# Two more units of the fifth group as seven products, their weight sums earlier, and other PSUM banks for the last two spectral chunks

## The chip, the cores and the metric

The kernel runs on one core of a Trainium2 chip. The core has a matrix engine (TensorE, "PE" in the profile, its weight loads "PEld"), a vector engine (VectorE, "DVE"), a scalar engine (ScalarE, "ACT"), GpSimd ("POOL") and a DMA-issuing queue (SyncE, "SP"). Each engine works through its own instructions in the order in which they stand; engines wait for each other with semaphores. The metric is the device time of one execution in microseconds. The kernel before takes 408.13 us (median of three runs, 408.11 to 408.33).

## The reference

The input x has 2048 tokens of 448 numbers. After a layer norm, two branches are added to it.

```
x  = A_x
xn = _layernorm(x, axis=-1)
A  = irfft2(rfft2(xn) * (w_r + 1j * w_i))          # over tokens and channels
h  = _gelu(_layernorm(xn, axis=-1) @ w1)           # 448 -> 448
hs = concatenate(four quarters of h, shifted by +1, -1, +2, -2 tokens) @ w2
x1 = xn + hs
B  = x1 + _gelu(_layernorm(x1, axis=-1) @ w3) @ w4 # 448 -> 1792 -> 448
out = x + A + B
```

## The kernel before

**Tiles and stages.** Tokens lie in 16 blocks `b` of 128, in the tiles `xt0` to `xt7` (two blocks each), which also collect the result. Products are made in half precision with a high and a low half of each factor, so that each product is three passes (`PASS`): high by high, high by low of the second factor, low of the first factor by high. A first stage makes h and x1 (`w1_unit`, `w2_tile`, `ln2`). Then come the two long parts, which are interleaved: the channel MLP (`mlp`), and the spectral branch, in order `do_fold` and `step1` (transform over channels), 16 chunks of frequencies (`chunk_a`, `chunk_b`, `chunk_z`, `chunk_c`), and the inverse transform of 16 blocks (`gather_u`, `inv_a`, `inv_b`).

**The MLP.** It goes by groups G = 0 to 7 of 256 tokens and, in each, by seven units fp, each of which is 256 of the 1792 hidden columns. `front(G, fp)` makes the hidden values: 22 matmuls into one PSUM bank `pw3_Gfp` (L400, `pw` in the profile), then a gelu on ACT (L726) and the two halves `hf` on ACT and DVE (L728, L729). `back(G, fp)` multiplies by w4: 12 matmuls of 448 columns into the two banks `acc` of the group (L808). The banks of the fronts, tag "mm", are two. `mlp` issues fronts one or two units ahead of backs.

**Units as seven products.** For the units in the table `SEVEN` the back is a two-by-two block product with seven half-width products in place of eight (`seven`, L763): 7 x 3 = 21 matmuls of 224 columns (L778). Three of the seven go into `acc`, four into two further banks per group, `side` (tag "sp" in the fifth group). The front of such a unit is `sums` (L733): gelu into a tile `g` (L738), two DVE additions (L740, L741), and the two halves `hz` on ACT and DVE (L744, L745). The tile `g` has two buffers and `hz` has three; a buffer is written again only when every reader of its earlier content is done. The weights also need sums: `w4_sums(j)` (L749) loads w4's rows of unit pair j by a DMA, makes four DVE additions (L757) and splits the result into halves on ACT (L280) and DVE (L281) into `w4t[j]`. Its places: j = 1 overwrites hidden inputs that groups 0 and 1 read, j = 2 and 3 those that groups 2 and 3 read. When the units of the group are done, DVE adds `side` and `acc` to `xt` (L786, L815).

**The spectral chunks.** Chunk c: `pp` (L622) into a bank of tag "tr", halves `pf` (L629, L630); `px` (L639) into a bank of tag "sp", then `te` (ACT L644, DVE L645, L646), `z` on POOL (L648), halves `zb` (L655, L656), and `pu` (L667) into a bank of tag "sp", from which ACT and DVE write `y1` (L670, L671). Tags "sp" and "tr" have two banks each. The inverse gathers `U` from `y1` (L680), makes `pe` (L688) in "tr", a chain of DVE steps (L695 to L699) with halves `vh` (L701, L702), then `py` (L709) in "sp", and adds it to `xt` (L711).

**What sets the order.** The order on each engine is not written out: a scheduler takes the ready instruction of highest priority, by its own estimate of times. MLP fronts and backs run at the lowest priority (`FILL`), so that they fill PE while the spectral branch waits. `behind(...)` makes an instruction follow others. Once built, the order is fixed.

Of the kernel before, what the change touches and what calls it, by code (L numbers as in the profile page):

```python
# [12 lines left out]
F32 = mybir.dt.float32  # L13
# [25 lines left out]
AFTER = [[], [3], [4], [5], [6], [7], [], []]  # L39
EVAC, FILL = 0, 100000  # L40
DH = D // 2
SEVEN = {5: [0, 4, 5], 6: [0, 4, 5, 1, 2, 3], 7: [0, 1, 2, 4, 5]}
ORD = {G: list(range(7)) for G in range(5)} | {5: [1, 2, 3, 6, 0, 4, 5], 6: [0, 4, 5, 1, 2, 3, 6],
                                               7: [0, 1, 2, 4, 5, 3, 6]}

ME = [0, 224] + list(range(2, 224, 2))
# [79 lines left out]
def body(tc, nc, x, wf, w1, w2, w3, w4, c_g, c_n, c_small, out):  # L126
# [14 lines left out]
    def pool(name, bufs=1, side="left", space=None):  # L141
        kw = dict(name=name, bufs=bufs, reuse_waits="tile")
        if space is not None:
            kw["space"] = space
        else:
            kw["side"] = side
        cm = tc.tile_pool(**kw)
        opened[name] = cm
        return cm.__enter__()

    def close(name):
        opened.pop(name).__exit__(None, None, None)
# [3 lines left out]
    def bank(tag, name):  # L156
        return ps.tile([128, 512], F32, tag=tag, bufs=2, name=name)

    pc = pool("pc")
    px = pool("px")  # L160
# [213 lines left out]
    @contextlib.contextmanager  # L374
    def behind(*key):
        key = key if len(key) > 1 else key[0]
        with contextlib.ExitStack() as st:
            for i in after[key]:
                st.enter_context(tc.issue_after(i))
            yield  # L380
# [141 lines left out]
    def finish(b):  # L522
        t = xb(b)
        if b < 2:
            t = row()[:, :D]
            SY.dma_start(t, xv[:, at_token(b)])
            V.scalar_tensor_tensor(out=t, in0=xb(b), scalar=p12, in1=t, op0=ALU.mult, op1=ALU.add)
        SY.dma_start(ov[:, at_token(b)], t)
# [54 lines left out]
    def w_scale_end():  # L583
        t = pc.tile([128, 4], F32, name="wt")
        V.tensor_reduce(out=t[:, 0:1], in_=wm, axis=AX.X, op=ALU.max)
        pt = bank("sp", "wpt")
        T.transpose(pt[0:1, 0:128], t[:, 0:1], ident)
        V.tensor_reduce(out=t[0:1, 1:2], in_=pt[0:1, 0:128], axis=AX.X, op=ALU.max)
        V.tensor_scalar(out=t[0:1, 1:2], in0=t[0:1, 1:2], scalar1=2.0 ** -20, scalar2=None, op0=ALU.max)
        pb = bank("sp", "wpb")  # L590
        T.matmul(pb[:, 0:1], ones[0:1], t[0:1, 1:2], start=True, stop=True)
        e = pc.tile([128, 3], I32, name="we")
        V.tensor_copy(out=t[:, 2:3], in_=pb[:, 0:1])
        V.tensor_single_scalar(e[:, 0:1], t.bitcast(I32)[:, 2:3], 0x7F800000, op=ALU.bitwise_and)
        V.tensor_single_scalar(e[:, 1:2], e[:, 0:1], 0x7F800000, op=ALU.bitwise_xor)
        V.tensor_scalar(out=sc[:, 0:1], in0=e.bitcast(F32)[:, 1:2], scalar1=ZPRE, scalar2=None, op0=ALU.mult)
        for h in range(2):
            V.tensor_scalar(out=sc[64 * h:64 * h + 64, 2:3], in0=sc[64 * h:64 * h + 64, 0:1], scalar1=2.0 * h - 1.0,
                            scalar2=None, op0=ALU.mult)
        V.tensor_scalar(out=sc[:, 1:2], in0=e.bitcast(F32)[:, 0:1], scalar1=2.0 ** -21 / (ZPRE * UPRE * VPRE),  # L600
                        scalar2=s12[:, 0:1], op0=ALU.mult, op1=ALU.mult)
        V.tensor_scalar(out=sc[:, 3:4], in0=sc[:, 1:2], scalar1=p12, scalar2=None, op0=ALU.mult)
# [30 lines left out]
    def chunk_b(c):  # L633
        w, k, _ = stream[c]
        pf = pfs.pop(c)
        px_ = bank("sp", f"px{c}")
        for h in range(2):
            for n, (pi, gi) in enumerate(PASS):
                T.matmul(px_[:, DF * h:DF * h + DF], k[:, gi, h], pf[:, pi, h], start=n == 0, stop=n == 2)  # L639
        src = px_[:, :2 * DF]  # L640
        o = stage(f"te{c}", 6 * DF, c % 2)
        e, t = o[:, :2 * DF], o[:, 2 * DF:].rearrange("p (a n) -> p a n", a=2)
        for h in range(2):
            A.activation(out=e[64 * h:64 * h + 64], in_=px_[64 - 64 * h:128 - 64 * h, :2 * DF], func=AF.Copy)  # L644
        V.scalar_tensor_tensor(out=t[:, 0], in0=src, scalar=sc[:, 0:1], in1=w[:, 0], op0=ALU.mult, op1=ALU.mult)  # L645
        V.scalar_tensor_tensor(out=t[:, 1], in0=e, scalar=sc[:, 2:3], in1=w[:, 1], op0=ALU.mult, op1=ALU.mult)  # L646
        z = pst.tile([128, 2 * DF], F32, tag="z", bufs=2, name=f"z{c}")
        P.tensor_tensor(out=z, in0=t[:, 0], in1=t[:, 1], op=ALU.add)  # L648
        zs[c] = z
# [8 lines left out]
    def chunk_c(c):  # L658
        _, _, k = stream.pop(c)
        zh = zb[c % 2]  # L660
        pu = bank("sp", f"pu{c}")
        for par in range(2):
            for h in range(2):
                d = pu[:, 256 * par:256 * par + 256].rearrange("p (q k) -> p q k", k=8)[:, :, 4 * h:4 * h + 4]
                for n, (zi, ki) in enumerate(PASS):
                    o = (2 * zi + h) * DF + 113 * par
                    T.matmul(d, zh[:, o:o + 128], k[:, ki, h].rearrange("p (q k) -> p q k", k=4), start=n == 0, stop=n == 2)  # L667
        src = pu[:113].rearrange("p (q n) -> p q n", q=4)
        d = [Y1[:113, p, :, c].rearrange("p q b k -> p q (b k)") for p in range(2)]
        A.activation(out=d[0], in_=src, func=AF.Copy, scale=UPRE)  # L670
        V.scalar_tensor_tensor(out=d[1], in0=src, scalar=UPRE, in1=d[0], op0=ALU.mult, op1=ALU.subtract)  # L671
# [44 lines left out]
    def front(G, fp, tag):  # L716
# [5 lines left out]
        with prio(EVAC):  # L722
            if fp in SEVEN.get(G, ()):
                hs[G, fp] = sums(G, fp, pm)
# [24 lines left out]
    def w4_sums(j, part):  # L749

        t = part.rearrange("p (k n) -> p k n", n=DH)
        SY.dma_start(t.rearrange("p (f k) n -> p f (k n)", f=2), w4v[:, 2 * j:2 * j + 2])

        def go():
            for o, i, k, op in ((3, 3, 1, ALU.subtract), (1, 1, 0, ALU.subtract),
                                (0, 3, 0, ALU.add), (2, 2, 0, ALU.subtract)):
                V.tensor_tensor(out=t[:, o], in0=t[:, i], in1=t[:, k], op=op)  # L757
            split_w(w4t[j][:, 0], w4t[j][:, 1], t, s4)
        return go
# [3 lines left out]
    def seven(G, fp, end):  # L763
        h = hs.pop((G, fp))
        lead, last = fp == SEVEN[G][0], fp == SEVEN[G][-1]
        if lead:
# [5 lines left out]
        t2, t1, t4, t3 = ([w4t[fp][:, i, k] for i in range(2)] for k in range(4))  # L772
        begins = fp == ORD[G][0]
        for blk, to, b, new in ((2, m1, w(0, 0), lead), (4, a1[:, 0:DH], w(1, 0), begins), (1, a2[:, 0:DH], t4, begins),
# [13 lines left out]
    def back(G, fp):  # L788
        first, end = fp == ORD[G][0], fp == ORD[G][-1]
        if first:  # L790
# [3 lines left out]
        h = None  # L794
        if fp in SEVEN.get(G, ()):
            seven(G, fp, end)
        else:
            h = hs.pop((G, fp))
        for i in range(2):
# [3 lines left out]
            for r, to in parts if h is not None else ():  # L803
                with behind("m", G, fp) if G == 7 and end and ("m", G, fp) in after else contextlib.nullcontext():
                    for f in (2 * fp, 2 * fp + 1):
                        for n, (hi, wi) in enumerate(PASS):
                            o = 256 * (f % 2) + 128 * i
                            m = T.matmul(to, h[:, hi, o:o + 128], w4p[0][:, wi, f, r],  # L808
                                         start=first and f % 2 == 0 and n == 0, stop=end and f % 2 == 1 and n == 2,
                                         skip_group_check=G in SEVEN)  # L810
                after["m", G, fp] = (m.ins,)
# [8 lines left out]
    def mlp(Gs, hook=None, ahead=1, tags=("mm",)):  # L820
        with prio(FILL):
            todo = [(G, fp) for G in Gs for fp in ORD[G]]
            done = 0
            for n, (G, fp) in enumerate(todo):
                while done < min(n + 1 + (ahead if todo[n] != (7, 5) else 1), len(todo)):
                    front(*todo[done], tags[done % len(tags)])
                    if hook:
                        with prio(EVAC):
                            hook(*todo[done])
                    done += 1  # L830
                back(G, fp)
# [57 lines left out]
    n = 2  # L889
# [148 lines left out]
    close("pfd")  # L1038
    with behind("m", 2, 3):
        w_scale_end()  # L1040
    pst = pool("pst", side="right")
    zb = [pst.tile([128, 4 * DF + 16], F16, name=f"zb{i}") for i in range(2)]
    for i in range(2):
# [10 lines left out]
            chunk_c(i - 3)  # L1054
    close("pst")
    mlp(range(3, 5))
    pv = pool("pv", side="right")
    bs = [*range(8), *range(12, 16), *range(8, 12)]
    for n in range(17):
        if n in (0, 8):  # L1060
            gather_u(n)
        if n < 16:
            inv_a(bs[n])
        if n:
            b = bs[n - 1]
            inv_b(b)
            if b < 10:
                finish(b)
    close("pa2")
    pz = pool("pz")  # L1070
    LATE = [(1, 5, 0), (2, 5, 5), (3, 6, 4)]

    def w4_late(G, fp):
        for n, (j, *at) in enumerate(LATE):
# [33 lines left out]
```

## Time and profile before

| | |
|---|---|
| median of three runs | 408.13 us |
| the profiled execution, its own time | 408.05 us |
| span of its instructions | 406.3 us |
| PE busy | 399.9 us (98%) |
| DVE busy | 333.6 us (82%) |
| ACT busy | 255.1 us (63%) |

The span counts from the first to the last instruction; 1.75 us lie around it. Times in rows are from the span's start. A matmul's end is modelled, and the next one starts before it, so what a matmul costs PE is read from the distance of starts, not from its duration. "idle before" is time in which the engine did nothing before an instruction, with what ended it.

### The profile page before, as it was taken

What the parts mean: (1) busy time and instruction counts of PE and PEld (TensorE: products, weight loads), DVE (VectorE), ACT (ScalarE), POOL (GpSimd) and SP (SyncE); (2) the same over time, 40 slices, a digit from 0 to 9 for tenths busy, and PEclk for the clock granted to TensorE, in tenths of its full rate; (3) what the DMA queues carried; (4) which work ended last, traced back from release to release, by engine and by line L of the source; (5) the groups of instructions that cost most, each with busy time, mean ns of one, the idle gap of its engine ahead of it and who ended that gap; (6) DMA issues with size and microseconds to landing.
All of it is one profiled execution on the core that took longest, in us unless ns stands there. A gap on an engine that the chain in (4) does not pass through costs nothing.

```text
span 406.3 us, 8732 instructions
## 1 busy us (share of the span) xinstructions
PE 399.9 (98%) x3391; PEld 297.2 (73%) x3391; DVE 333.6 (82%) x702; ACT 255.1 (63%) x433; POOL 100.4 (25%) x158
## 2 busy tenths in 40 slices
PE   8999999999999999999999999999999999999996
PEld 3555555865667877777878878777677779998995
DVE  5898799898947887988698888965999999965645
ACT  4788889874568857655698878853354544353431
POOL 6859910111146946500021111110000000000000
PEclk9999999999999999999999999999999999999999
DMA  8978975567489661637256556510011023100101
GB/s 280 389 272 160 249 152 138 122 121 163 95 225 266 234 191 46 219 95 185 72 144 164 162 142 161 139 27 2 24 69 70 24 90 92 47 2 2 45 2 45
DMA packets 54596, 52.07 MB, mean 128 GB/s; under 512 B 35678, under 2 KB 48542, under 8 KB 54556
## 3 DMA queue, kind: packets, MB, share of 16 engines
q1 hardware_dynamic: 54556, 51.53, 46.0%
q8 instruction: 26, 0.43, 0.4%
q14 instruction: 14, 0.11, 0.1%
HBM read 38.28 MB, written 3.67 MB: 103 GB/s over the span
## 4 chain that ended last, share of the span: by engine, by line
PE 87%; POOL 5%; DMA 2%; DVE 2%; ACT 2%; issue 1%; SPq 0%; POOLq 0%; ACTq 0%
PE pw L400 33%; PE acc L808 23%; PE pw L478 6%; PE side L778 4%; PE acc L778 3%; PE pu L667 3%; PE ps L567 3%; PE pe L688 2%; PE pp L622 2%; PE px L639 2%; PE py L709 2%; PE pw L420 2%; DMA w1s<-w 1%; POOL xt L336 1%; DMA h<-x2mem 1%
## 5 line engine op out<-in xcount | busy, mean ns | idle before, releaser
L400 PE MATMUL pw<-x2mem,w3p 128*128 128x256 f16 x1232 | 151.3, 273 | 0.0
L400 PEld LDWEIGHTS <-w3p 128*128 128x128 f16 x1232 | 118.9, 98 | 19.3
L808 PE MATMUL acc<-w4p,hf 128*128 128x448 f16 (+1 forms) x516 | 104.4, 348 | 0.0
L808 PEld LDWEIGHTS <-hf 128*128 128x128 f16 x516 | 50.1, 98 | 37.6
L726 ACT ACTIVATE pw<-pw,pe 128x512 f32<-128x512 f32 x42 | 27.4, 654 | 26.8 <-PE pw L400 26.6
L729 DVE SCALAR_TENSOR_TENSOR hf<-pw,h,hf 128x512 f16<-128x512 f32 x42 | 31.3, 746 | 12.9 <-ACT hf L728 12.7
L478 PE MATMUL pw<-w2p,h 128*128 128x448 f16 x176 | 35.8, 353 | 0.9 <-DMA h<-x2mem 0.9
L420 PE MATMUL pw<-w1p,xT 128*128 128x448 f16 x176 | 34.9, 352 | 0.1
L648 POOL TENSOR_TENSOR z<-te 128x450 f32<-128x450 f32 x16 | 15.7, 983 | 70.8 <-DVE te L646 65.9
L728 ACT ACTIVATE hf<-pw,h 128x512 f16<-128x512 f32 x42 | 28.9, 687 | 5.0 <-PE acc L808 4.0
L478 PEld LDWEIGHTS <-h 128*128 128x128 f16 x176 | 17.0, 98 | 17.0 <-DMA h<-x2mem 2.0
L744 ACT ACTIVATE hz<-g,h 128x896 f16<-128x896 f32 x14 | 14.6, 1044 | 23.1 <-DVE g L741 23.1
L420 PEld LDWEIGHTS <-xT 128*128 128x128 f16 x176 | 17.1, 99 | 16.1 <-DVE xT L394 0.4
L778 PEld LDWEIGHTS <-hz 128*128 128x128 f16 x294 | 28.3, 98 | 0.6
L629 ACT ACTIVATE pf<-pp 64x450 f16<-64x450 f32 x32 | 17.4, 544 | 12.5 <-DVE pf L630 9.7
L630 DVE TENSOR_TENSOR pf<-pp,pf 64x450 f16<-64x450 f32 x32 | 19.9, 622 | 5.1 <-ACT pf L629 4.7
L745 DVE SCALAR_TENSOR_TENSOR hz<-g,h,hz 128x896 f16<-128x896 f32 x14 | 16.1, 1148 | 6.8 <-ACT hz L744 6.8
L550 POOL TENSOR_TENSOR f<-xr 128x452 f32<-128x452 f32 x16 | 19.7, 1251 | 0.6
L558 DVE TENSOR_TENSOR xh<-f,xh 128x452 f16<-128x452 f32 x16 | 14.3, 916 | 5.7 <-ACT xh L557 5.7
L644 ACT ACTIVATE te<-px 64x450 f32<-64x450 f32 x32 | 17.3, 541 | 1.2 <-PE px L639 0.6
L738 ACT ACTIVATE g<-pw,pe 128x512 f32<-128x512 f32 x14 | 9.6, 683 | 11.3 <-PE pw L400 11.3
L547 POOL TENSOR_TENSOR xr<-xf 128x452 f32<-128x452 f32 x8 | 9.2, 1156 | 22.3 <-issue 16.4
(188 smaller groups left out, 705.7 us busy)
## 6 DMA issues: line engine op xcount, KB each, us to landing
wc<-wf SPq DMA_DIRECT2D x32, 225.0 KB, 3.7
wl<-wf SPq DMA_DIRECT2D x8, 450.0 KB, 4.3
xt<-x SPq DMA_DIRECT2D x8, 448.0 KB, 7.1
xf<-x SPq DMA_DIRECT2D x8, 448.0 KB, 4.6
loads<-x SPq DMA_DIRECT2D x7, 448.0 KB, 4.0
out<-xt SPq DMA_DIRECT2D x13, 224.0 KB, 1.9
w3raw<-w SPq DMA_DIRECT2D x3, 896.0 KB, 10.8
gn<-c_g SPq DMA_DIRECT2D x16, 128.0 KB, 3.0
```

What stands on the lines that cost most here:

```text
L400: T.matmul(ps_out, wp[:, wi + t, cols], xT[:, xi + t, tok], start=t == 0 and wi + xi == 0, stop=t == 3 and wi == 4)
L420: m = T.matmul(pm[:, :D], xTs[g][:, xi + t, 128 * i:128 * i + 128], w1p[:, wi + t], start=t == 0 and p == 0, stop=t == 3 and p == 2)
L478: T.matmul(pm[:, :D], h[:, k], w2p[:, w], start=n == 0, stop=n == 10)
L550: P.tensor_tensor(out=f[:, :, k:k + 2].rearrange("p b s d -> p s b d"), in0=u[:, :, 0], in1=u[:, :, 1], op=op)
L629: A.activation(out=hi, in_=src, func=AF.Copy)
L630: V.tensor_tensor(out=lo, in0=src, in1=hi, op=ALU.subtract)
L644: A.activation(out=e[64 * h:64 * h + 64], in_=px_[64 - 64 * h:128 - 64 * h, :2 * DF], func=AF.Copy)
L726: A.activation(out=pm, in_=pm, func=AF.Gelu_apprx_tanh, scale=r3)
L728: i = A.activation(out=h[:, 0], in_=pm, func=AF.Copy, scale=h3)
L729: j = V.scalar_tensor_tensor(out=h[:, 1], in0=pm, scalar=h3, in1=h[:, 0], op0=ALU.mult, op1=ALU.subtract)
L778: m = T.matmul(to, h[:, hi, 128 * blk:128 * blk + 128], b[wi], start=new and n == 0, stop=n == 2 and (last if blk in (2, 5, 3, 0) else end ...
L808: m = T.matmul(to, h[:, hi, o:o + 128], w4p[0][:, wi, f, r], start=first and f % 2 == 0 and n == 0, stop=end and f % 2 == 1 and n == 2, sk ...
```

## The change

- `SEVEN[5]` gets the units 1 and 2: five units of the fifth group go as seven products. `ORD[5]` puts the two plain units first (3, 6), then 0, 4, 5, 1, 2.
- Half sums of w4 for j = 1 are made in the third group, behind its unit 1, through a tile `early` of a new pool `pt`; they were made in the fifth group before. Those for j = 2 come behind unit (5, 6), and those for j = 3 behind unit (6, 0).
- In chunks 14 and 15 the banks `px` and `pu` are taken from tag "tr" (the banks of `pp`) in place of "sp".

```diff
-SEVEN = {5: [0, 4, 5], 6: [0, 4, 5, 1, 2, 3], 7: [0, 1, 2, 4, 5]}
-ORD = {G: list(range(7)) for G in range(5)} | {5: [1, 2, 3, 6, 0, 4, 5], 6: [0, 4, 5, 1, 2, 3, 6],
+SEVEN = {5: [0, 4, 5, 1, 2], 6: [0, 4, 5, 1, 2, 3], 7: [0, 1, 2, 4, 5]}
+ORD = {G: list(range(7)) for G in range(5)} | {5: [3, 6, 0, 4, 5, 1, 2], 6: [0, 4, 5, 1, 2, 3, 6],
                                                7: [0, 1, 2, 4, 5, 3, 6]}
...
-        px_ = bank("sp", f"px{c}")
+        px_ = bank("tr" if c in (14,15,) else "sp", f"px{c}")
...
-        pu = bank("sp", f"pu{c}")
+        pu = bank("tr" if c in (14,15,) else "sp", f"pu{c}")
...
+    pt = pool("pt")
     pst = pool("pst", side="right")
...
     mlp(range(3, 5))
+    for n, j in enumerate((1,)):
+        with behind(*(("f", 3,1), ("f", 4,5))[n]):
+            w4_sums(j, pt.tile([128, 896], F32, tag="early", bufs=1, name=f"early{j}"))()
...
+    close("pt")
     close("pa2")
     pz = pool("pz")
-    LATE = [(1, 5, 0), (2, 5, 5), (3, 6, 4)]
+    LATE = [(2,5,6),(3,6,0)]
```

The two engines below show where the built order moves. In names, `hz51` is the tile hz of group 5, unit 1; the number behind the underscore is the program's own.

DVE in the chunk stage, behind the low half of unit (3, 1), before:

```order
L729 SCALAR_TENSOR_TENSOR hf31_3492<-pw3_31_3468,h3_666,hf31_3492 128x512
L656 TENSOR_TENSOR zb1_2541<-z1_2647,zb1_2541 128x450
L630 TENSOR_TENSOR pf4_2725<-pp4_2712,pf4_2725 64x2x225
L656 TENSOR_TENSOR zb0_2540<-z2_2688,zb0_2540 128x450
L671 SCALAR_TENSOR_TENSOR y1_1548<-pu0_2690,y1_1548 113x4x128
L645 SCALAR_TENSOR_TENSOR te3_2739<-px3_2732,sc_138,wc3_2649 128x450
```

and now:

```order
L729 SCALAR_TENSOR_TENSOR hf31_3495<-pw3_31_3471,h3_666,hf31_3495 128x512
L757 TENSOR_TENSOR early1_3998<-early1_3998 128x224
L656 TENSOR_TENSOR zb1_2544<-z1_2650,zb1_2544 128x450
L630 TENSOR_TENSOR pf4_2728<-pp4_2715,pf4_2728 64x2x225
L656 TENSOR_TENSOR zb0_2543<-z2_2691,zb0_2543 128x450
L757 TENSOR_TENSOR early1_3998<-early1_3998 128x224
L671 SCALAR_TENSOR_TENSOR y1_1548<-pu0_2693,y1_1548 113x4x128
```

The additions of `early` stand between the chunk's steps; two more of them and the split L281 follow within the next nine rows.

PE at the end of the fifth group, from the last matmul that reads `hz50` to the first that reads the buffer's next content, before (the last row is the 57th matmul behind the first):

```order
L778 MATMUL side51_4695<-x2mem_119,hz50_4641 128x224
L778 LDWEIGHTS hz54_4691
...
L400 MATMUL pw3_65_4874<-x2mem_119,w3p_132 128x256
L778 LDWEIGHTS hz60_4833
L778 MATMUL side60_4906<-w4p_991,hz60_4833 128x224
```

and now (the last row is the 13th matmul behind the first):

```order
L778 MATMUL side51_4629<-x2mem_119,hz50_4583 128x224
L778 LDWEIGHTS hz54_4625
...
L778 MATMUL side51_4629<-w4p_991,hz55_4678 128x224
L778 LDWEIGHTS hz51_4729
L778 MATMUL side50_4628<-w4p_991,hz51_4729 128x224
```

The buffer of `hz50` was handed to `hz60`, a unit of the next group, behind 56 other matmuls; now it is handed to `hz51`, and 12 matmuls on `hz54` and `hz55` stand between. Eight matmuls on the high half of `hz51` follow before the first on its low half.

ACT at the same place now:

```order
L701 ACTIVATE vh11_4462<-e11_4456 128x448
L280 ACTIVATE x2mem_119<-late2_4534,pe4_984 128x896
L744 ACTIVATE hz51_4729<-g51_4725,h3_666 128x896
L744 ACTIVATE hz52_4780<-g52_4776,h3_666 128x896
L738 ACTIVATE g60_4857<-pw3_60_4834,pe3_662 128x2x2x128
```

The halves of units 1 and 2 stand behind the last `vh` of the inverse and ahead of the first gelu of the sixth group.

## The prediction, made before the changed kernel was run

> **What bounds the kernel now.** I read the page first (busy times, slices, chain), then the waits of PE, then windows over the part that the change touches.
>
> ```profile
> span 406.3 us, 8732 instructions
> PE 399.9 (98%) x3391; PEld 297.2 (73%) x3391; DVE 333.6 (82%) x702; ACT 255.1 (63%) x433; POOL 100.4 (25%) x158
> PE   8999999999999999999999999999999999999996
> PE 87%; POOL 5%; DMA 2%; DVE 2%; ACT 2%; issue 1%; SPq 0%; POOLq 0%; ACTq 0%
> ```
>
> PE is busy in every slice and is 87% of the chain that ends last. Its waits from 51 us to the end are one row:
>
> ```profile
> PE pw L478 <- DMA h<-x2mem: 0.2, 1, 0.2
> ```
>
> So behind 51 us PE has no hole that a better order could fill. The time can only fall by what PE no longer streams, and any new hole in PE is paid in full. The windows show who has room beside it (columns: busy and instruction count of each engine, then clock, DMA share, GB/s):
>
> ```profile
> core 0: us, PE busy (x) PEld busy (x) DVE busy (x) ACT busy (x) POOL busy (x), PEclk, DMA share, GB/s
> 195.00:215.00 20.00, 20.00 (x209) 16.30 (x207) 18.01 (x29) 17.36 (x32) 3.94 (x4) 1.00 0.48 130
> 215.00:235.00 20.00, 20.00 (x229) 16.90 (x228) 17.47 (x29) 16.70 (x31) 3.94 (x4) 1.00 0.61 157
> 300.00:315.00 15.00, 15.00 (x140) 11.01 (x138) 14.86 (x38) 6.48 (x13) 0.00 (x0) 1.00 0.17 63
> 330.00:345.00 15.00, 15.00 (x141) 13.42 (x139) 13.99 (x28) 7.67 (x10) 0.00 (x0) 1.00 0.34 108
> ```
>
> In the chunk stage DVE and ACT have 2.0 to 3.3 us of room in 20. In the inverse DVE is 93 to 99% busy, yet always in time, for PE stands at 15.00 of 15.00.
>
> **What PE saves.** One front lies between two backs here, so the distance of starts gives the price of a back:
>
> ```profile
> 362.71 2.57 PE L400 MATMUL pw<-x2mem,w3p 128*128 128x256 f16 x22
> 365.11 0.45 PE L778 MATMUL side<-w4p,hz 128*128 128x224 f16 x3
> ...
> 367.12 2.57 PE L400 MATMUL pw<-x2mem,w3p 128*128 128x256 f16 x22
> ...
> 371.54 2.56 PE L400 MATMUL pw<-x2mem,w3p 128*128 128x256 f16 x22
> 373.94 2.43 PE L808 MATMUL acc<-w4p,hf 128*128 128x448 f16 x12
> 376.21 2.57 PE L400 MATMUL pw<-x2mem,w3p 128*128 128x256 f16 x22
> ```
>
> A plain back is 376.21 - 373.94 = 2.27 us (189 ns a matmul), one as seven products 367.12 - 365.11 = 2.01 us (96 ns). A front costs 2.40 either way. Two units change: 2 x 0.26 = **0.52 us saved**. The rest of PE's matmuls are the same ones.
>
> The Trainium skill, "TensorE: Matmul & The Clock Gate", section "Back-to-back issue gap", speaks against the change: in a stream of weight load and matmul pairs it gives about 81 ns a matmul of 128 columns and about 131 ns of 512. Between them, my estimate from that page is 121 ns at 448 and 93 ns at 224 columns; 12 would then cost 1.45 us and 21 cost 1.95, so the change would lose 1.0 us on PE. The trace has 189 and 96 ns and does not agree for the long ones, and the sum goes by the trace.
>
> **The new hole: the buffers of hz.** The tile hz has three buffers. Units 0, 4, 5 of the fifth group hold them until their products into `side` are done, and those wait for the `py` banks, that is, for the end of the inverse. Before, the fourth user was unit (6, 0), and 56 matmuls stood between:
>
> ```profile
> 341.05 1.31 PE L778 MATMUL side<-x2mem,hz 128*128 128x224 f16 x12
> ...
> 342.77 1.03 PE L778 MATMUL side<-w4p,hz 128*128 128x224 f16 x9
> 343.63 3.98 PE L400 MATMUL pw<-x2mem,w3p 128*128 128x256 f16 x35
> 347.45 0.35 PE L778 MATMUL side<-w4p,hz 128*128 128x224 f16 x2
> ```
>
> Now it is `hz51`, and from the start of the last matmul on `hz50` to that of the first on the low half of `hz51` PE has 21 matmuls (the last itself, 12 on the other two, 8 on the high half): 21 x 0.096 = 2.01 us. Against this stand, in a chain, the release, the high half on ACT, the low half on DVE and the weight load. Nothing else fills the hole: front (6, 5) stands behind it in the order, and needs a bank that the gelu of (6, 0) frees, which itself waits for a buffer of g that this low half frees. The durations, and three hand-overs (PE to DVE, ACT to DVE, DVE to the weight load):
>
> ```profile
> L744 ACT ACTIVATE hz<-g,h 128x896 f16<-128x896 f32 x14 | 14.6, 1044 | 23.1 <-DVE g L741 23.1
> L745 DVE SCALAR_TENSOR_TENSOR hz<-g,h,hz 128x896 f16<-128x896 f32 x14 | 16.1, 1148 | 6.8 <-ACT hz L744 6.8
> L778 PEld LDWEIGHTS <-hz 128*128 128x128 f16 x294 | 28.3, 98 | 0.6
> ```
>
> ```profile
> 338.01 0.35 PE L709 MATMUL py<-vh,csm 128*128 128x448 f16 x1
> 338.40 0.69 DVE L711 SCALAR_TENSOR_TENSOR xt<-py,sc,xt 128x448 f32<-128x448 f32 x1 [0.33 <-PE py L709]
> 355.70 1.04 ACT L744 ACTIVATE hz<-g,h 128x896 f16<-128x896 f32 x1 [2.70 <-DVE g L741]
> 356.77 1.15 DVE L745 SCALAR_TENSOR_TENSOR hz<-g,h,hz 128x896 f16<-128x896 f32 x1 [0.89 <-ACT hz L744]
> 9.33 0.16 DVE L258 TENSOR_REDUCE pt<-m 128x1 f32<-128x4 f32 x1 [0.47 <-ACT xr L253]
> 9.54 0.30 PEld L260 LDWEIGHTS pm<-pt,ones 128*128 128x128 f32 x2 [0.86 <-DVE pt L258]
> ```
>
> A short L778 matmul ends 0.26 us behind its start (the rows of two last 0.35, one pitch more). The chain: 0.26 + 0.04 (338.40 less 338.36) + 1.04 + 0.03 (356.77 less 356.74) + 1.15 + 0.05 (9.54 less 9.49) + 0.10 for the load = 2.67 us. Less 2.01, PE stands still for **0.66 us**, some 0.2 of it at the high half and the rest at the low one. The bounds: without load and hand-overs 0.44; with both halves' loads laid bare 0.76. I take 0.66, since PE cannot load weights that do not exist yet. Below zero it cannot go. `hz52` is 1.0 us behind on ACT and 2.0 on PE, so it makes no second hole; behind it front (6, 5) covers.
>
> **The rest of the edits, at nothing.** Sums of w4 for j = 1 go into the chunk stage:
>
> ```profile
> 336.05 0.62 DVE L702 SCALAR_TENSOR_TENSOR vh<-e,vh 128x448 f16<-128x448 f32 x1
> 336.58 0.42 DVE L740 TENSOR_TENSOR g<-g 128x256 f32<-128x256 f32 x1
> 336.92 0.39 DVE L757 TENSOR_TENSOR late<-late 128x224 f32<-128x224 f32 x1
> 337.22 0.55 DVE L741 TENSOR_TENSOR g<-g 128x384 f32<-128x384 f32 x1
> 337.68 0.39 DVE L757 TENSOR_TENSOR late<-late 128x224 f32<-128x224 f32 x1
> 344.61 1.14 DVE L745 SCALAR_TENSOR_TENSOR hz<-g,h,hz 128x896 f16<-128x896 f32 x1
> 345.68 1.14 DVE L281 SCALAR_TENSOR_TENSOR x2mem<-late,pe,x2mem 128x896 f16<-128x896 f32 x1
> ```
>
> By starts, an L757 takes 0.30 and a split as long as an L745 1.07, so four and one are 2.3 us on DVE, with 1.03 on ACT (an L280 is of L744's size). The windows have 2.0 and 2.5 us of DVE room just there, so the chunks fall behind by up to 2 us and catch up. PE's order already holds these chunk products about 1 to 2 us later and runs fronts first; walking the changed rows with these durations, the tightest hand-overs of a "sp" bank keep 0.9 us. If that cover is gone, `pu` and `px` are late next. The DMA for `early` is one more issue on SP, ahead of the transposes of `y8`:
>
> ```profile
> 96.71 1.25 SPq L514 DMA_TRANSPOSE x2mem<-y  x1
> ...
> 104.78 5.24 SPq L514 DMA_TRANSPOSE x2mem<-y  x4
> L420 PE MATMUL pw<-w1p,xT x176: 349/352/362, 11.7 to 67.8; 128*128 128x448 f16 x176
> ```
>
> SP idles there from 98.0 to 104.78, and the memory that it waits for is last read at 67.8 us, so it costs nothing.
>
> The other banks for chunks 14 and 15 let their `pu` and the inverse start earlier: along the changed order the first `pe` has one back (2.27) and 14 front matmuls (1.53) less ahead of it, 3.8 us. PE was full there, so this gains nothing by itself. DVE needs it: ahead of the last `vh` come three more pairs of additions (3 x 0.80) and one L745 more (1.07), two plain low halves (2 x 0.67) and two L757 less, +1.5 us. The last `vh` thus comes 2.3 us sooner and PE wants it some 2.2 sooner. The margin now, 338.01 less 336.67, is 1.3 us, and stays so.
>
> **The sum.** Profiled execution 408.05 - 0.52 + 0.66 = 408.19 us; the median of the runs is 0.08 higher. I forecast 408.2: no change.
>
> **Rivals.**
> - *The hole is small.* If matmuls end sooner than modelled, or the load hides, the stall falls towards 0.44 or less: 407.6 (no stall) to 407.9. For it: ends are modelled. Against it: the two halves alone, 1.04 + 1.15 = 2.19 us, already exceed the 2.01.
> - *DVE falls behind in the chunk stage, slower.* 2.3 us of work stand among steps that free "sp" banks with 0.9 us to spare; if the chunks are late by all of it once, PE waits 2.3 - 0.9 = 1.4 us: 409.6. It decides from 0.7 us on (408.19 + 0.7 is 0.2% above the median). For it: ACT is as full as DVE there. Against: PE has fronts to run.
> - *Short matmuls cost their weight load.* If loads (98 ns) held up the long series on `hz`, each of 42 would pay more; at 1.0 us lost in place of 0.52 gained the time is 409.7. The row of 21 in 2.01 us speaks against it.
> - *Faster.* The lead of 3.8 us in the inverse pays somewhere. This needs PE holes that can close, and the waits show 0.2 us: at best 407.3.
>
> **How the numbers follow.** The forecast (407.95 to 408.5) gets 0.58, the small hole 0.16, late chunks 0.17, the dear load 0.02, faster 0.05, slower in an unnamed way 0.02. A measurement of this kernel tells 0.2% (0.8 us) from no change, so the first two are both "same": faster 0.05, same 0.74, slower 0.21. The range is 407.5 (no stall) to 409.2 (half of the late chunks' cases).
>
> **What would show it.** PE's waits should have a new row of some 0.2 us on ACT `hz` and one of 0.4 on DVE `hz`, near 340 us, and no other; L808 should have 24 matmuls less and L778 42 more; L744 of `hz51` should be released by PE `side`. Waits of `pu`, `px` or `py` on DVE from 207 to 336 us, or none at 340, would make the prediction wrong.

## The result, and the profile after

The changed kernel takes 409.05 us (median of 19 runs, 408.50 to 409.60); the kernel before takes 408.06 in the same comparison (19 runs, 407.57 to 408.42). The ratio is 1.0022, 95% interval 1.0015 to 1.0028: slower by 0.2%, at the edge of what can be told from no change. The profiled execution took 408.64 us, against 408.05 before.

From the page of the changed kernel, its span, its busy times and the shares of the chain:

```profile
span 406.9 us, 8770 instructions
PE 400.0 (98%) x3409; PEld 298.9 (73%) x3409; DVE 335.9 (83%) x706; ACT 256.1 (63%) x433; POOL 100.2 (25%) x158
PE 85%; POOL 5%; DVE 3%; DMA 2%; ACT 2%; issue 2%; SPq 1%; ACTq 0%; POOLq 0%
```

PE still bounds the kernel, but its busy time, 400.0, is no smaller than the 399.9 of before, though 42 short matmuls replace 24 long ones. Behind the first stage, PE's waits show two rows, where the kernel before has none:

```profile
PE side L778 <- DVE hz L745: 0.2, 1, 0.2
PE pu L667 <- DMA gn<-c_n: 0.2, 1, 0.2
```

That is not all that PE lost. The end of a matmul is modelled, so a stop shorter than the modelled tail of the matmul ahead (0.26 us for 224 columns, against 0.096 from start to start) shows no idle time; the row that holds it is only too long. So I measured stops by starts: for each matmul, the distance to the next start less the usual distance for its shape, where the excess is over 0.04 us. In us, from 195 us to the end, with four of the experiments beside it:

| place | before | after | e1 | e3 | e4 | e12 |
|---|---|---|---|---|---|---|
| `px`, 232 to 240 | 0.07 | 0.12 | 0.14 | 0.07 | 0.14 | none |
| `pp`, 247 to 248 | 0.05 | 0.15 | 0.15 | 0.05 | 0.16 | 0.04 |
| `pu` or `px`, 261 to 262 | none | 0.13 | 0.13 | 0.89 | 0.07 | none |
| `pu`, 266 to 269 | none | 0.35 | 0.20 | none | none | none |
| `hz51`, 341 to 342 | none | 0.62 | none | no `hz51` | no `hz51` | none |
| sum | 0.12 | 1.37 | 0.63 | 1.01 | 0.36 | 0.04 |

Rows of two of the stops in the chunk stage, of the changed kernel:

```profile
231.01 0.69 DVE L645 SCALAR_TENSOR_TENSOR te<-px,sc,wc 128x450 f32<-128x450 f32 x1
231.75 0.74 PE L639 MATMUL px<-pf,gn 128*128 128x225 f16 x6
...
267.07 0.72 PE L667 MATMUL pu<-gn,zb 128*128 128x128 f16 x10
267.99 0.27 PE L667 MATMUL pu<-gn,zb 128*128 128x128 f16 x2 [0.19 <-DMA gn<-c_n]
```

At 231.75 PE starts 0.05 us behind the end of the DVE step that frees its bank; the stops at 248.25 and 261.59 end in the same way, 0.06 and 0.05 us behind an L630 and an L645. At 267.99 it is the inputs: ten matmuls from 267.07 should have led to 267.63.

The profiled executions then add up: 0.52 saved, 1.26 of new stops (1.37 against 0.12), 0.19 less lost ahead of 51 us (5.21 against 5.40 by the same measure, in stages that the change does not touch): +0.55, and the last matmul starts 0.57 us later (403.32 for 402.75). Of the 1.26, 0.62 is the stop that the prediction named and 0.64 lies in the chunk stage, where it had put nothing.

The stop at `hz51`, on PE, ACT and DVE (the time lines of the changed kernel):

```profile
339.23 1.31 PE L778 MATMUL side<-x2mem,hz 128*128 128x224 f16 x12
340.38 1.15 PE L778 MATMUL side<-w4p,hz 128*128 128x224 f16 x8
...
341.75 0.35 PE L778 MATMUL side<-x2mem,hz 128*128 128x224 f16 x2
342.35 0.27 PE L778 MATMUL side<-w4p,hz 128*128 128x224 f16 x1 [0.24 <-DVE hz L745]
```

```profile
340.07 1.98 ACT L744 ACTIVATE hz<-g,h 128x896 f16<-128x896 f32 x2 [2.29 <-PE side L778]
```

```profile
341.14 2.21 DVE L745 SCALAR_TENSOR_TENSOR hz<-g,h,hz 128x896 f16<-128x896 f32 x2 [2.18 <-ACT hz L744]
```

ACT sat idle for 2.29 us until PE released the buffer; DVE then sat for ACT. Eight matmuls take 1.15 us where 7 x 0.096 + 0.26 = 0.93 is usual: the 0.21 at the high half. From 341.75 two matmuls should have led to 341.94; the low half starts at 342.35: 0.41.

The last 0.4 us of the 0.99 between the medians is not in this trace. Each run has its span and its time. Outside the span the kernel before spends 1.65 to 1.77 us (21 runs beside the first experiments, median 1.73); the changed kernel 1.74 to 2.59 (median 1.95). The median span is 407.0 against 406.4. e10 below takes this up.

### The profile page after: what moved, and what is told of

It reads as the page before. It is cut to its first block, busy times and chain, and to the rows that moved or that the text cites. A ratio compares the mean times of both kernels' runs of the same rounds, so it can differ in the third digit from the quotient of the medians.

```text
span 406.9 us, 8770 instructions
## 1 busy us (share of the span) xinstructions
PE 400.0 (98%) x3409; PEld 298.9 (73%) x3409; DVE 335.9 (83%) x706; ACT 256.1 (63%) x433; POOL 100.2 (25%) x158
## 4 chain that ended last, share of the span: by engine, by line
PE 85%; POOL 5%; DVE 3%; DMA 2%; ACT 2%; issue 2%; SPq 1%; ACTq 0%; POOLq 0%
PE pw L400 33%; PE acc L808 22%; PE pw L478 6%; PE side L778 4%; PE acc L778 3%; PE ps L567 3%; PE pp L622 2%; PE pe L688 2%; PE pu L667 2%; PE py L709 2%; PE pw L420 2%; PE px L639 2%; DMA w1s<-w 1%; POOL xt L336 1%; POOL w2p L278 1%
## 5 line engine op out<-in xcount | busy, mean ns | idle before, releaser
L400 PE MATMUL pw<-x2mem,w3p 128*128 128x256 f16 x1232 | 151.4, 273 | 0.0
L400 PEld LDWEIGHTS <-w3p 128*128 128x128 f16 x1232 | 119.1, 98 | 19.7
L808 PE MATMUL acc<-w4p,hf 128*128 128x448 f16 (+1 forms) x492 | 101.0, 348 | 0.0
L808 PEld LDWEIGHTS <-hf 128*128 128x128 f16 x492 | 47.4, 98 | 34.3
L726 ACT ACTIVATE pw<-pw,pe 128x512 f32<-128x512 f32 x40 | 26.0, 652 | 25.7 <-PE pw L400 25.6
L729 DVE SCALAR_TENSOR_TENSOR hf<-pw,h,hf 128x512 f16<-128x512 f32 x40 | 29.7, 743 | 11.7 <-ACT hf L728 11.5
L420 PE MATMUL pw<-w1p,xT 128*128 128x448 f16 x176 | 34.7, 352 | 0.0
L778 PEld LDWEIGHTS <-hz 128*128 128x128 f16 x336 | 32.1, 98 | 1.4 <-DVE hz L745 0.5
L728 ACT ACTIVATE hf<-pw,h 128x512 f16<-128x512 f32 x40 | 27.4, 685 | 4.9 <-PE acc L808 4.0
L420 PEld LDWEIGHTS <-xT 128*128 128x128 f16 x176 | 17.1, 99 | 15.8 <-DVE xT L394 0.4
L738 ACT ACTIVATE g<-pw,pe 128x512 f32<-128x512 f32 x16 | 11.0, 687 | 22.1 <-PE pw L400 21.5
L745 DVE SCALAR_TENSOR_TENSOR hz<-g,h,hz 128x896 f16<-128x896 f32 x16 | 18.2, 1147 | 7.8 <-ACT hz L744 7.8
L744 ACT ACTIVATE hz<-g,h 128x896 f16<-128x896 f32 x16 | 16.3, 1038 | 12.1 <-DVE g L741 9.1
L630 DVE TENSOR_TENSOR pf<-pp,pf 64x450 f16<-64x450 f32 x32 | 19.9, 622 | 4.0 <-ACT pf L629 3.6
L778 PE MATMUL acc<-w4p,hz 128*128 128x224 f16 x105 | 15.3, 259 | 0.0
```

The costliest lines, as they stand in the source:

```text
L400: T.matmul(ps_out, wp[:, wi + t, cols], xT[:, xi + t, tok], start=t == 0 and wi + xi == 0, stop=t == 3 and wi == 4)
L420: m = T.matmul(pm[:, :D], xTs[g][:, xi + t, 128 * i:128 * i + 128], w1p[:, wi + t], start=t == 0 and p == 0, stop=t == 3 and p == 2)
L630: V.tensor_tensor(out=lo, in0=src, in1=hi, op=ALU.subtract)
L726: A.activation(out=pm, in_=pm, func=AF.Gelu_apprx_tanh, scale=r3)
L728: i = A.activation(out=h[:, 0], in_=pm, func=AF.Copy, scale=h3)
L729: j = V.scalar_tensor_tensor(out=h[:, 1], in0=pm, scalar=h3, in1=h[:, 0], op0=ALU.mult, op1=ALU.subtract)
```

## The experiments

Each was timed beside the kernel before, which took 408.10 (e1 to e4), 408.15 (e5 to e7), 408.25 (e8 to e10) and 408.04 us (e11, e12) at the median there.

### e1: a fourth buffer of hz

```diff
-        h = pz.tile([128, 2, 7 * 128], F16, tag="hz", bufs=3, name=f"hz{G}{fp}")
+        h = pz.tile([128, 2, 7 * 128], F16, tag="hz", bufs=4, name=f"hz{G}{fp}")
```

> The changed kernel with four buffers of hz in place of three, nothing else. Theory: the two stops of PE near 341 us (0.21 on the high half, 0.41 on the low half of hz51) are the wait for the buffer that unit (5, 0) holds; both go, no other stop appears there, and the time falls by 0.62 us, from 409.05 to about 408.4. The high half of hz51 then starts on ACT well ahead of the last product on hz50. Rival: ACT or DVE are late for hz51 for another reason (their queues are full behind the inverse); then the stops stay, or move to a neighbouring unit, and the time stays within 0.2 us of 409.05.

408.43 us, ratio 1.0006 (0.9997 to 1.0015): 0.62 less than the changed kernel, as expected. PE's time line at the place:

```profile
340.12 1.50 PE L778 MATMUL side<-x2mem,hz 128*128 128x224 f16 x14
341.46 0.74 PE L778 MATMUL side<-w4p,hz 128*128 128x224 f16 x6
342.04 0.83 PE L778 MATMUL side<-x2mem,hz 128*128 128x224 f16 x7
342.71 1.47 PE L400 MATMUL pw<-x2mem,w3p 128*128 128x256 f16 x12
```

Fourteen matmuls take 13 x 0.096 + 0.26 = 1.51: no stop. The wait for a buffer has moved on by one unit (ACT again waits 2.1 us for PE, at 341.09), but there PE has a front of L400 to run. The stop is the buffer's, and this is shown.

### e2: the banks of chunks 14 and 15 undone

```diff
-        px_ = bank("tr" if c in (14,15,) else "sp", f"px{c}")
+        px_ = bank("sp", f"px{c}")
...
-        pu = bank("tr" if c in (14,15,) else "sp", f"pu{c}")
+        pu = bank("sp", f"pu{c}")
```

> The changed kernel with px and pu of chunks 14 and 15 back in the banks sp. PE's order is the same as in the changed kernel up to pu of chunk 11 (260 us). Theory (the other banks cost time, since PE reaches pu of chunk 14 before the matrix that it needs has landed): the stops at 261.4 (0.13) and 267.6 us (0.35) go, the two near 341 stay; 409.05 - 0.48 = 408.6. Rival (the prediction's reading: the banks cost nothing and give DVE its lead): the last vh then comes late, PE waits for py of block 11 by 1 us or more, and the time is 409.6 or above.

412.73 us, ratio 1.0113 (1.0099 to 1.0127). My theory fell: the stops near 261 and 268 us did shrink to 0.07 and the one at `hz51` went, but 4.5 us came in elsewhere. The time is one that the rival allowed, but PE stops at `py` for only 0.3 us and ahead of `side` for 0.3 and 2.2. The time line of DVE, and windows of PE (columns as in the prediction's windows):

```profile
337.55 0.61 DVE L702 SCALAR_TENSOR_TENSOR vh<-e,vh 128x448 f16<-128x448 f32 x1
339.92 1.24 DVE L757 TENSOR_TENSOR late<-late 128x224 f32<-128x224 f32 x3 [1.76 <-DMA late<-w]
341.08 0.68 DVE L711 SCALAR_TENSOR_TENSOR xt<-py,sc,xt 128x448 f32<-128x448 f32 x1
```

```profile
339.40:342.50 3.10, 1.04 (x11) 0.79 (x10) 2.07 (x5) 0.41 (x1) 0.00 (x0) 1.00 0.59 172
342.50:346.00 3.50, 3.50 (x22) 2.76 (x20) 2.83 (x3) 3.08 (x4) 0.00 (x0) 0.51 0.00 0
```

DVE is not overworked here: it stands still for 1.76 us. In its order three additions on `late2` stand ahead of the L711 of block 11 that frees the last `py` bank; their data land at 339.90, and PE has only products into `side` left, which need that bank. PE stops for 2.2 us, and then the granted clock falls to 0.51: for 3.4 us matmuls of 224 columns start 0.187 us apart in place of 0.096, which costs another 1.6 us. So the other banks do not gain time; they keep the inverse ahead of a late transfer.

The Trainium skill, "TensorE: Matmul & The Clock Gate", section "What's actually happening", has the clock go to half after an idle window of about 3.4 us. The half clock agrees; here it came after one stop of 2.2 us, in a stretch in which PE was busy for 1.04 of 3.10 us.

### e3: the banks alone

```diff
-        px_ = bank("sp", f"px{c}")
+        px_ = bank("tr" if c in (14,15,) else "sp", f"px{c}")
...
-        pu = bank("sp", f"pu{c}")
+        pu = bank("tr" if c in (14,15,) else "sp", f"pu{c}")
```

> The kernel before, with px and pu of chunks 14 and 15 in the banks tr and nothing else. Theory (banks cost time by the matrix of chunk 14): PE's order brings pu of chunk 14 to about 266.2 us, and its matrix can be there at about 267.4 (released by pu of chunk 12 at 261.8, then 5.5 us for queue and transfer): a stop of 0.4 to 1.2 us there, none elsewhere; 408.5 to 409.3. Rival (prediction: PE is full, the banks move nothing): 408.1, no stop.

408.91 us, ratio 1.0023 (1.0013 to 1.0032). The size was as expected, the place was not. PE's time line:

```profile
259.85 1.50 PE L667 MATMUL pu<-gn,zb 128*128 128x128 f16 x24
262.08 0.74 PE L639 MATMUL px<-pf,gn 128*128 128x225 f16 x6 [0.73 <-DVE pf L630]
```

The free bank lets `px` of chunk 15 into the order right behind `pu` of chunk 12, where its `pf` is not there yet: 0.89 us. `pu` of chunk 14 waits for nothing. The banks cost because a product that no longer waits for a bank waits for its data, and what stands behind it in PE's order waits with it.

### e4: the early half sums alone

The added lines are those of the change (the pool `pt`, and the sums for j = 1 behind front (3, 1)), and:

```diff
-    LATE = [(1, 5, 0), (2, 5, 5), (3, 6, 4)]
+    LATE = [(2, 5, 5), (3, 6, 4)]
```

> The kernel before, with the half sums of w4 for j = 1 moved to the third group and nothing else (no banks, three units as seven products). Theory: the small stops in the chunk stage (0.12 at 231.6 and 0.15 at 248 us, where the kernel before has 0.07 and 0.05) come from these sums on DVE and ACT: 408.06 + 0.15 = 408.2. Rival: the sums make the chunks late by more, and the stops at 261 and 268 us are theirs too: 408.06 + 0.64 = 408.7.

409.33 us, ratio 1.0032 (1.0020 to 1.0043). Neither forecast came true. The stops are near those of the theory, 0.25 more than before (0.36 against 0.12), and the last matmul starts only 0.11 us later than before. The rest, 1.1 us, lies behind the last matmul. The end of the view of DMA issues, from 402 us, of e4:

```profile
out<-xt SPq DMA_DIRECT2D x1, 224.0 KB, 2.0
out<-xt SPq DMA_DIRECT2D x2, 112.0 KB, 2.4
```

In the kernel before the second row reads 1.8. The last transfer lands 2.89 us after its issue in place of 1.73, and the packets show a load of code (8 KB, on queue 14) that begins at 405.19, among its last packets. In the kernel before that load comes at 407.0, in the changed one at 401.6, both clear of it. In every other trace here the last transfer lands 1.72 to 1.75 us after its issue.

### e11: the same, with eight more small instructions on ACT and nine on DVE at the start

```diff
     V.memset(m2, 0.0)
+    pad = pc.tile([128, 2], F32, name="pad")
+    V.memset(pad, 0.0)
+    for _ in range(8):
+        V.memset(pad[:, 0:1], 0.0)
+        A.activation(out=pad[:, 1:2], in_=pad[:, 1:2], func=AF.Copy)
```

> The kernel of e4_early_alone with nine tiny memsets on DVE and eight tiny copies on ACT more at the start, PE's order the same. In e4 the last transfer landed 2.89 us after its issue (1.73 in the kernel before), and a code load of 8 KB on queue 14 began at 405.19 us, among its last packets. Theory (that load held up the end of the transfer): with more instructions the load falls some us earlier, the transfer lands after 1.73 again, and what is left of e4's loss is its stops: 408.15 + 0.25 = 408.4. Rival (the tail belongs to something else in that program): 2.9 again, 409.3.

409.16 us, ratio 1.0022 (1.0012 to 1.0032), but for other reasons. The tail is as expected: the code load has moved to 400.5, the last transfer lands after 1.73 us, and the same view gives again

```profile
out<-xt SPq DMA_DIRECT2D x2, 112.0 KB, 1.8
```

The stops of the chunk stage stayed (0.33). What took the gain back is a stop of 0.75 at 144.7 us and a later start of the first products (the first L420 at 12.25 us for 11.69), neither in e4, so the total time says nothing; the shortest of the 12 runs took 408.20. That the tail is long only where the load falls among the last packets is shown; by what means the load lengthens it, and that it alone makes e4's excess, is not.

### e5: a third buffer for the second matrix

```diff
-            k.append(pst.tile([128, 2, 2, 128], F16, tag=f"gn{i}", bufs=2, name=f"gn{i}_{c}"))
+            k.append(pst.tile([128, 2, 2, 128], F16, tag=f"gn{i}", bufs=2 + i, name=f"gn{i}_{c}"))
```

> The changed kernel with three buffers in place of two for the second matrix of each chunk (c_n, read by pu). PE's order is the same, matmul for matmul. Theory: PE stops 0.35 us in pu of chunk 14 (267.6 us) because its matrix landed at 267.85; with a third buffer its transfer no longer waits for pu of chunk 12, that stop goes, the one of 0.13 at 261.4 and the two near 341 stay: 409.05 - 0.35 = 408.7. Rival: the stop is the zb of chunk 14, not its matrix; then it stays and the time stays at 409.05.

409.04 us, ratio 1.0024 (1.0013 to 1.0036): no gain that can be told. The wait for the DMA is gone, but 0.19 of the 0.35 stays, and the rows of weight loads name the next input (window 260 to 270):

```profile
L667 PEld LDWEIGHTS <-zb 128*128 128x128 f16 x48 | 3.0, 98 | 0.5 <-DVE zb L656 0.2 <-issue 0.2
```

Both the theory and the rival held in part: `pu` of chunk 14 is pulled so far ahead that its matrix and its `zb` come within 0.2 us of each other, and taking one away leaves the other. In e1, too, with two buffers and PE's order the same up to 335 us, this stop was 0.20, so 0.15 of it can change without a third buffer.

### e6: e2 with the sums for j = 2 early as well

```diff
-    for n, j in enumerate((1,)):
+    for n, j in enumerate((1, 2)):
...
-    LATE = [(2,5,6),(3,6,0)]
+    LATE = [(3, 6, 0)]
```

and the banks as in e2.

> The changed kernel with chunks 14 and 15 back in the banks sp, as in e2_banks_undone, and the half sums for j = 2 also made early, in the early buffer (behind front (4, 5)) and not in the memory of the inverse. Theory A (in e2 DVE stood in front of the additions on late2, whose transfer landed at 339.90, with the step that frees the bank of py for block 11 behind them): the stop of 2.2 us and the slow matmuls behind it go; what stays is the hole of 0.62 at hz51 and 0.36 in the chunk stage, and the time is 408.06 - 0.52 + 0.62 + 0.25 = 408.4. Theory B (without the lead from the other banks DVE has too much work ahead of the last vh): DVE now has 1.2 us more there, so PE waits for vh or py by at least 2 us, and the time is above 411.

409.95 us, ratio 1.0041 (1.0028 to 1.0054): between the theories. The stop of 2.2 us and the half clock are gone, so they were the queue behind `late2`. What remains there are waits for DVE and ACT:

```profile
337.21 0.81 PE L709 MATMUL py<-vh,csm 128*128 128x448 f16 x3 [0.41 <-ACT vh L701]
338.20 0.35 PE L709 MATMUL py<-vh,csm 128*128 128x448 f16 x1 [0.19 <-DVE vh L702]
338.80 0.45 PE L778 MATMUL side<-w4p,hz 128*128 128x224 f16 x3 [0.25 <-DVE xt L711]
```

By starts 1.46 us, and `hz51` keeps its stop (0.56).

### e7: hz4, banks undone, both sums early, in the fourth group

The edits of e1 and e6, and the places of the sums:

```diff
-        with behind(*(("f", 3,1), ("f", 4,5))[n]):
+        with behind(*(("f", 4, 2), ("f", 4, 5))[n]):
```

> The five units as seven products, with four buffers of hz, chunks 14 and 15 in the banks sp, and the half sums for j = 1 and 2 early but in the fourth group (behind fronts (4, 2) and (4, 5)), so that PE's order in the chunk stage is that of the kernel before. Theory (each hole found so far is separate, and nothing replaces them): 408.06 - 0.52 = 407.5 to 407.6. Rival (DVE in the inverse has no room for 4.6 us of sums; its margin ahead of the last vh was 1.3 us): PE waits for vh or hz by 1 to 3 us, 408.6 to 411.

409.12 us, ratio 1.0024 (1.0016 to 1.0033). The rival holds. The chunk stage has one stop of 0.05, no more than in the kernel before; the inverse has three, two of them in these rows:

```profile
339.93 0.55 PE L709 MATMUL py<-vh,csm 128*128 128x448 f16 x2 [0.26 <-DVE xt L711]
...
343.94 1.31 PE L778 MATMUL side<-x2mem,hz 128*128 128x224 f16 x12 [0.78 <-DVE xt L711]
```

By starts 0.43 + 0.20 + 0.94 = 1.57 us of waits for DVE. In this order DVE has no room in the inverse for two sets of sums.

### e8 and e9: the sums on POOL

Both have e1's and e5's buffers and both sums early, behind fronts (4, 1) and (4, 5), with additions, scaling and low half on POOL. e8 has only `pu` of chunk 14 in a bank `tr`; e9 has all four as in the change.

```diff
-                V.tensor_tensor(out=t[:, o], in0=t[:, i], in1=t[:, k], op=op)
-            split_w(w4t[j][:, 0], w4t[j][:, 1], t, s4)
+                (E or V).tensor_tensor(out=t[:, o], in0=t[:, i], in1=t[:, k], op=op)
+            split_w(w4t[j][:, 0], w4t[j][:, 1], t, s4, E)
```

> The changed kernel with four buffers of hz, three for the second matrix of a chunk, only pu of chunk 14 in a bank tr (the rest in sp), and the half sums for j = 1 and 2 made on POOL, which is idle in the inverse, behind fronts (4, 1) and (4, 5). Theory (what the five units save on PE is lost only to holes, and those in the inverse are DVE's work, 2.3 us a set of sums): PE's order in the chunk stage is nearly that of the kernel before, no stop there; DVE has the last vh ready 4.6 us ahead of PE by durations alone (4.0 in the kernel before), so no stop of py or side; 408.15 - 0.52 = 407.6, a ratio of 0.9987. Rival (POOL beside DVE slows both, or the ACT part of the split holds up the queue ahead of vh): a stop of 0.5 to 1.5 us at py or hz51, 408.1 to 409.1.

> As e8_pool_one_bank, but px and pu of chunks 14 and 15 all in the banks tr, as in the changed kernel. Theory: px of chunk 15 stands at 262.0 us in PE's order, and e3_banks_alone showed that it can start at 262.1 at the earliest, so a stop of 0.1 to 0.3 us; pu of chunk 14 at 266.8 waits up to 0.2 us for its zb; the inverse has 5.5 us of lead and no stop; 408.15 - 0.52 + 0.4 = 408.0. Rival (the lead of 2 us over e8 is worth more than the stops): 407.6 or below.

409.62 us, ratio 1.0039 (1.0025 to 1.0053), and 409.39, ratio 1.0031 (1.0019 to 1.0042). Neither theory held, and e8's rival only in its kind. The time lines of POOL and of DVE in e8:

```profile
266.92 0.66 POOL L757 TENSOR_TENSOR early<-early 128x224 f32<-128x224 f32 x1 [3.68 <-DMA early<-w]
267.54 0.98 POOL L648 TENSOR_TENSOR z<-te 128x450 f32<-128x450 f32 x1
268.48 2.57 POOL L757 TENSOR_TENSOR early<-early 128x224 f32<-128x224 f32 x3
271.16 1.01 POOL L276 TENSOR_SCALAR early<-early,pe 128x896 f32<-128x896 f32 x1
```

```profile
269.17 0.63 DVE L656 TENSOR_TENSOR zb<-z,zb 128x450 f16<-128x450 f32 x1 [2.86 <-ACT zb L655]
...
271.37 1.27 DVE L646 SCALAR_TENSOR_TENSOR te<-te,sc,wc 128x450 f32<-128x450 f32 x1
```

POOL is idle in the inverse, but the order put the sums for j = 2 among the last chunks. POOL stood 3.68 us for their transfer with a `z` behind it: a queue behind a late transfer as in e2, on another engine. DVE then waits 2.86 us at the next `zb`, 2 us later than in the kernel before (267.22). And while POOL runs L276, an L646 takes 1.27 us, where others take 0.68. So the last `zb` is 1.5 us late and `pu` at 274 stops twice, 0.45 us in all; the rest of e8's 1.7 us of stops is a `py` at 287 (0.34) and an `acc` and a `pe` near 305 (0.87 together), whose causes I did not follow. e9 pays 0.72 at `px` of chunk 15 and 0.70 at 270 us, the second for a `zb` whose `z` stood behind sums on POOL again; its waits name the inputs:

```profile
PE px L639 <- DVE pf L630: 0.6, 1, 0.6
PE pu L667 <- ACT zb L655: 0.5, 1, 0.5
```

### e10: eighteen more matmuls of one column

In the kernel before:

```diff
     warm_up(WARM)
+    for _ in range(18):
+        T.matmul(wps[:, 0:1], wsrc[:, 0:128], wsrc[:, 0:1], start=True, stop=True)
```

> The kernel before with 18 more matmuls of one column behind the warm-up, where PE waits for more than 3 us anyway, so that PE has as many instructions as in the changed kernel (3409 matmuls). Theory (the time outside the profiled span, 1.73 us in the kernel before and 1.95 at the median in the changed one, grows by a further load of PE's code at the end): the span stays at 406.4 us, the time outside it rises to about 1.9, and the time to 408.3. Rival (it is not the number of PE's instructions): 1.73 outside, 408.1.

408.70 us, ratio 1.0015 (1.0004 to 1.0026). The theory had 408.3. The median span is 406.4 (406.6 in the kernel before beside it), and outside it the 11 runs spend 1.67 to 2.99 us, median 2.0, against 1.65 to 1.74 in the 15 runs of the kernel before beside them. So a PE program that is 36 instructions longer costs time that no row of the span shows, 0.3 us at the median and over 1 us at times. The other programs bear this out: those with 3391 matmuls (e3, e4, e11) spend at most 1.85 us outside the span in any run, while each one with 3409, the changed kernel and the others, has runs above 2.1. That this is PE's code being loaded at the end is not settled: a further load of 16 KB, on the queue that I take for PE's (8), appears in some profiles (at 408.0 in e1, with 2.33 outside), but e5 has one too with 1.86, and e9 none with 2.07.

### e12: hz4, a third matrix buffer, only pu in the other banks, the sums in the inverse

```diff
-        px_ = bank("tr" if c in (14,15,) else "sp", f"px{c}")
+        px_ = bank("sp", f"px{c}")
...
-        with behind(*(("f", 3,1), ("f", 4,5))[n]):
+        with behind(*(("f", 4, 4), ("f", 4,5))[n]):
```

with the edits of e1 and e5.

> The changed kernel with four buffers of hz, three for the second matrix of a chunk, only pu of chunks 14 and 15 in the banks tr (px in sp), and the sums for j = 1 on DVE in the inverse, behind front (4, 4). Theory: PE's order in the chunk stage is that of the kernel before up to pu of chunk 12, so no stop there; DVE has the last vh 4.2 us ahead by durations alone, as in the kernel before (4.0), so at most 0.3 us of stops at py; 408.15 - 0.52 + 0.3 + 0.2 outside the span = 408.1. Rival (the additions on late2 stand ahead of the step that frees the last py bank, and their transfer lands at 337 to 338 us): PE waits 1 us or more at side, 409 or above.

407.60 us against 408.04, ratio 0.9994 (0.9985 to 1.0002): lower by 0.44 at the median, with an interval that still holds no change. It is 0.5 below the theory's 408.1, which had allowed 0.3 for stops at `py`. The profile is clear. Its span, and a window over the place of the old stop:

```profile
span 405.8 us, 8774 instructions
```

```profile
330.00:345.00 15.00, 15.00 (x140) 13.33 (x139) 11.57 (x24) 5.92 (x8) 0.00 (x0) 1.00 0.27 93
```

Behind 195 us one stop of 0.04 is left, and the span is 0.5 us shorter than before: the saving of the two units, whole. The median span of the 12 runs is 405.8 against 406.3; outside it they spend 1.92 against 1.72, as e10 has it for PE's longer program.

## Why the prediction came out as it did

The forecast was 408.2 and "no change"; the time is 409.05, inside the range, and past the bound of 0.2% by a little, on the slower side. It is above the band that the forecast gave itself (407.95 to 408.5) and among the cases that it called slower, 0.21 in all. That the range holds it is in part luck: it reached up to 409.2 for one long wait, and what filled it were several short ones and time outside the span, none of them in the sum. By its own sign of being wrong (waits of `pu`, `px` or `py` on DVE from 207 to 336 us) the prediction had the chunk stage wrong: read by starts, `px` at 231.75 and `pu` at 261.59 wait for DVE. By its steps:

- **PE bounds, every hole is paid in full: right.** All the time that came or went inside the span, in all runs but e4, is a stop of PE, its half clock, or a later start of its first products (e8, e11).
- **0.52 us saved: right.** e12 has the same 3409 matmuls and no new stop, and is 0.5 us shorter in span. By the prediction's estimate from the Trainium skill, "TensorE: Matmul & The Clock Gate", section "Back-to-back issue gap", PE would have lost 1.0 us (a straight line between that section's figures gives 123 ns at 448 columns, not 121, and the same loss). e12 does not agree with it, and agrees with the rows of 2.27 and 2.01 us.
- **The hole at `hz51`, 0.66: right in place and cause, measured 0.62.** e1 removes it; of the other stops only that of `pu` differs there (0.20 for 0.35). The split was 0.21 and 0.41, as forecast (some 0.2, the rest). The waits show only 0.2 of it, so "a row of 0.2 on ACT and one of 0.4 on DVE" was wrong as a test: the short distance of starts against the long modelled tail hides them.
- **Early sums, "at nothing": wrong, 0.25 us** (e4, by stops). The step that failed is "the chunks fall behind by up to 2 us and catch up", with a margin of 0.9 at the tightest bank. The stop near 232 us is PE waiting for the bank that L645 frees: L645 ends at 231.70, and `px` starts at 231.75. This stop and that at 248 stand 17 and 33 us behind the end of the split, so I take it that the changed order there is a little tight, and not that DVE is full while it adds; no run separates the two. In e7, e9 and e12, with the sums elsewhere, none above 0.05 is left at these places.
- **Other banks, "gains nothing by itself": right on the gain, wrong on the price, about 0.4 us.** 0.76 of stops in the chunk stage less e4's 0.36 leaves 0.39. I walked the releases of the banks and not the arrival of what the moved products read: matrix, `zb`, `pf`. e3 shows it most plainly, 0.89 for `pf`.
- **"DVE needs it": right, but for half the reason.** Without the banks the kernel takes 412.73 (e2). Most of the loss in e2 is a transfer in front of DVE's queue and the half clock after it. DVE's work is short as well: 0.56 us of stops, waits for two L711, come ahead of that one in e2, and 1.46 are left in e6. That e6's number is near the count of +1.5 us is no proof of it, since e6 moves further sums.
- **The margin ahead of the last `vh` stays: right.** The changed kernel has no stop at `py` or `vh`. The size was off on the safe side: the last `vh` ends at 334.01 and PE's last `py` starts at 336.33, so the margin is 2.3 us, not 1.3.
- **Outside the span: not thought of.** The sum took the kernel before's 0.08 between profile and median as given. It grew to 0.4, of which the runs show 0.2 to 0.3 as time outside the span; e10 makes PE's longer program the likely reason.

The rival "late chunks" named the right stage, and for three of its four stops the right engine, but as one wait of 1.4 us; they came as 0.12 to 0.35 each, and the largest is a wait for the matrix and `zb`.

## What to carry to other kernels

When PE is full, a change that removes matmuls is worth their distance of starts (0.52 us here, which e12 shows), and it is worth it only if nothing that it reorders arrives late: list for each product that moves forward every input and every bank, and what stands ahead of their makers in DVE's, ACT's, POOL's and SP's order, above all anything that waits for a transfer. Count short stops by the starts of matmuls, since a view of waits leaves out those that a modelled tail covers. A difference of half a microsecond between two programs can also lie outside the span, or in a code load that meets the last transfer, so compare spans and the time outside them apart.

## What the runs showed of the hardware that I had not expected

- After a stop of 2.2 us the granted clock was 0.51 for 3.4 us, and the distance of matmuls of 224 columns went from 0.096 to 0.187 us (e2). The stops of 0.9 us in e3 and e7 left it at 1.00.
- Eighteen tiny matmuls in a place where PE was idle did not lengthen the span (406.4 us, 406.6 without them) and added 0.3 us outside it at the median, with a spread from 1.67 to 2.99 (e10).
- Where a code load of 8 KB began 1.5 us after the last output's issue, that transfer landed after 2.89 us in place of 1.73 (e4); with the load shifted by some instructions it landed after 1.73 again (e11).
- Two steps of DVE with both inputs in SBUF took nearly twice as long beside POOL's work on 896 columns: an L646 1.27 us for 0.68, ending 0.47 us behind POOL's L276, and an L656 1.18 for 0.63, ending 0.48 behind L278 (e8). Steps that read a bank of PSUM beside the same L278 kept their time (L630 0.63). The Trainium skill, "SBUF — State Buffer", section "Who interferes with whom", has a DVE step with two SBUF inputs contend with a POOL step that reads SBUF, over shared ports that only one of them can have at a time. The numbers agree that the two contend; both steps ended 0.15 to 0.2 us sooner behind POOL's than a step of their own length would have, had it begun only then.
